# A gated mix of two attentions: the output and late-query products as 64-row halves inside the score bursts

## The chip, the cores and the metric

One core of one Trainium2 chip runs the whole program. The metric is device microseconds of that core, the median over several executions. Engines are called TensorE (PE, its weight loads PEld), VectorE (DVE), ScalarE (ACT), GpSimd (POOL) and SyncE (SP, which issues most DMAs).

## The reference

The output is `g * a + (1 - g) * b` for a sequence of 2048 tokens of 512 features, 32 heads of 16. All inputs and the output are float32.

```python
x = A_x                                                   # 1 x 2048 x 512
g = _sigmoid((x * gate_w).sum(-1, keepdims=True))
# a: full softmax attention
q, k, v = ((x @ wqkv) split into 3, by heads)
a = softmax(q k^T * 0.25) v, heads joined, @ A_wo
# b: four segments of 512 tokens, each attends causally to itself and reads a memory of the segments before it
for s in range(4):
    a_dot = softmax(qs ks^T * 0.25 + causal mask) vs
    a_mem = (phi(qs) M) / (phi(qs) z + 1e-6)              # phi(t) = t + 1 where t > 0, else exp(t)
    o_s   = sigmoid(beta) * a_mem + (1 - sigmoid(beta)) * a_dot
    M, z  = M + phi(ks)^T vs, z + sum(phi(ks))
b = (o_0 .. o_3 joined) @ B_wo
```

## The kernel before

A first phase (about 0 to 281 us) projects queries, keys and values, stores them to device memory, and builds the memory of side B. The attention follows, cut into units `(side, g, c)`: four heads `g`, one chunk `c` of 512 queries. Sides alternate, A then B, 32 of each. A unit of side A has 64 slots (`SLOTS`), one of side B has 10. A slot is one score tile: 128 keys by 512 queries of one head. Each slot does these things:

- `score_part(n)`: TensorE multiplies keys by queries into one of three rotating banks (`st`, line 1045), and ScalarE takes the exponential into a tile `p` (lines 1065 and 1068). On side B, GpSimd blanks what lies above the diagonal.
- `max_part(m)`, for the slot `LEAD` = 96 ahead: TensorE makes a tile with the operands exchanged (`sm`, line 242, four banks), and VectorE takes the row extremes (line 275, with a mask line 290). They are subtracted later inside the score product, through two additional rows of its operands.

Query and key tiles hold two heads in partitions 0 to 63 and two in 64 to 127. A product uses only 48 or 50 rows of one half. Score and maximum of one slot lie in opposite halves, so the two run side by side in TensorE.

Slots go in bursts of three (`BURST`). After each burst TensorE does something of another shape, which goes to the eighth bank, `ops`:

- `some_values(n, most(n))`: values times `p` (line 155, `ops<-p,vA` and `ops<-p,vB`, 128 rows by 17 columns, four heads side by side). `queue` holds slots whose exponentials are due; `most(n)` says how many are taken, three or four in most bursts. At a unit's end ScalarE copies `ops` to `oraw` (line 1106), and it is stored.
- Or, while the list `shared` holds anything, three items of it (line 155, 128 rows by 128 columns by 512). When side A's unit ends, `some_values` extends `shared` by twelve such products: either `output(...)`, half of one 128-token block of the final projection (operands `wA`, `wB` and `blk`; ended by `keep` or `leave`, which copy `ops` out on ScalarE, lines 1259 and 1263), or `later_tile(...)`, a query tile that the first phase left out (`ops<-wB,wA`, copy on line 962). Each logical product is three of high and low parts.

So twelve products take four bursts, during which no values are taken. The order is fixed in the program, each engine goes through its instructions in order, and waits follow from the tiles. `wait_early` ties the loads of the next burst to the last matmul of a burst; `run_late` transposes finished maxima. `wide`, the last 94 slots, is ordered otherwise, and the change does not touch it.

Of the kernel before, what the change touches and what calls it, by code (L numbers as in the profile page):

```python
# [10 lines left out]
F32 = mybir.dt.float32  # L11
F32R = mybir.dt.float32r
AF = mybir.ActivationFunctionType
ALU = mybir.AluOpType
# [8 lines left out]
CH = 512  # L23
# [11 lines left out]
LEAD = 96  # L35
BURST = 3
# [3 lines left out]
NP = 6  # L40
# [7 lines left out]
def gated_mix(ctx, tc, x, xT, wqkv, a_wo, b_wq, b_wk, b_wv, b_wo, beta, gate_w, out):  # L48
    nc = tc.nc
# [7 lines left out]
    for side in "AB":  # L57
        for o in range(NO):
            for c in range(NCH):
                rows_ = [32, 8, CH] if side == "A" else [2, 8, DH, CH]  # L60
# [22 lines left out]
                            compare_op=ALU.is_ge, fill=0.0)  # L83
    nc.gpsimd.affine_select(out=heads8, in_=heads8, pattern=[[DH, 8]], base=DH - 1, channel_multiplier=-1,
                            compare_op=ALU.is_ge, fill=0.0)
# [67 lines left out]
    def matmul(*args, **kw):  # L153

        behind[0] = nc.tensor.matmul(*args, **kw)  # L155
# [149 lines left out]
    def run_todo(m):  # L305

        for e in [e for e in todo if e[0] <= m]:
            todo.remove(e)
            e[1]()

    def run_late(pool, tag, m):
        while us := [e for e in late if e[0] < m][:2]:
            for e in us:
                late.remove(e)
            transpose_max(us, pool, tag)
# [639 lines left out]
    def x_later(c):  # L955
        return xT[:, c * CH:(c + 1) * CH]

    def later_tile(c, o):

        def done():  # L960
            full = fr.tile([128, CH], F32, tag="part", name="full")
            nc.scalar.copy(full, ops)
            t = fr.tile([128, 2, 2, 2, 128], F32R, tag="blk", name="qhalves", bufs=2)
            t = t.rearrange("p a o h t -> p a (o h t)")
            nc.gpsimd.tensor_copy(t[:, 0], full)
            nc.gpsimd.tensor_sub(t[:, 1], full, t[:, 0].bitcast(F32))
            for i in range(2):
                at(n + 12, lambda i=i: nc.sync.dma_start(
                    qd["A", o, c][16 * i:16 * i + 16].rearrange("d h t -> (d h) t"), raw(t[:, i])))


            if o == NO - 1 and c == LATER[0]:
                for i in range(2):
                    load_halves(("x", LATER[1]), "B", x_later(LATER[1]), (2 * i, 2 * i + 1), n + 2 + 18 * i,
                                [n + 24 + 29 * i, n + 28 + 29 * i])
            elif o == NO - 1:
                for i, (side, w) in enumerate((("A", a_wo), ("B", b_wo))):
                    load_halves(side, side, w, (0, 1), n + 2 + 18 * i, [n + 22 + 8 * i, n + 26 + 8 * i])
                    for k in range(2, 4):
                        load_halves(side, side, w, (k,), n + 50 + 22 * i + 3 * (k - 2), [n + 62 + 18 * i + 5 * (k - 2)])  # L980

        def f(i):
            k, (a, b) = i // 3, ((1, 0), (0, 1), (0, 0))[i % 3]
            assert {("q", k), (("x", c), k)} <= ready
            matmul(ops, halved["q"][:, k, a, o * 128:(o + 1) * 128], halved["x", c][:, k, b],
                             start=(i == 0), stop=(i == 11))
            if i == 11:
                done()
        for i in range(12):
            yield lambda i=i: f(i)  # L990

    vt = {}

# [33 lines left out]

    queue = []

    def score_part(n):  # L1030

        u, j = slots[n]
        side, g, c = u
        q = qt[u]

        if j % 4 == 0:
            pt_[u, j // 4] = pp.tile([128, 4, CH], F32, tag="p", name="p")
            order_p[u, j // 4] = len(order_p)
            assert not queue or order_p[queue[0][1], queue[0][2] // 4] > len(order_p) - 1 - NP
        p = pt_[u, j // 4]  # L1040
        h = (0, 2, 1, 3)[j % 4]

        def score(ps, h, b, k, n0, q0):

            nc.tensor.matmul(ps[:, n0:n0 + CH - q0], rows(k[:, :, b * 128:(b + 1) * 128], h, 50),  # L1045
                             rows(q[:, :, q0:], h, 50), start=True, stop=True)

        def diagonal(x):
            nc.gpsimd.affine_select(out=x, in_=x, pattern=[[0, 4], [1, 128]], base=0, channel_multiplier=-1,  # L1049
                                    compare_op=ALU.is_ge, fill=0.0)  # L1050

        ps = banks[1 + n % BURST] if n in wide and n // BURST % 2 else st_ps.tile([128, CH], F32, tag="st", name="st")
        if side == "A":
            score(ps, h, j // 4 % 4, kt_[u, j // 16], 0, 0)
        else:
            k = kt_[u, c]
            if j < 8:
                score(ps, h, j // 4, k, 0, 128 * (j // 4))
                if j >= 4:
                    score(ps, h, 3, k, 384, 384)  # L1060
            else:
                for f in range(2):
                    score(ps, 2 * (j - 8) + f, 2, k, 256 * f, 256)
        if side == "B" and j >= 8:
            nc.scalar.activation(p[:, 2 * (j - 8):2 * (j - 8) + 2, 0:256], ps.rearrange("p (h t) -> p h t", h=2), AF.Exp,
                                 scale=SCALE)
        else:
            nc.scalar.activation(p[:, h], ps, AF.Exp, scale=SCALE)  # L1068
        if j % 4 == 3 or j == SLOTS[side] - 1:
            if side == "B":  # L1070
                diagonal(p[:, :, 0:128])
                if j == 7:
                    diagonal(p[:, :, 384:])
            queue.extend((n + (2 * BURST * (1 + (side == "B")) if n in wide else GAP[side]), u, i) for i in range(j // 4 * 4, j + 1))


    PIECES = ([(0, 128 * i, 128 * i) for i in range(4)] + [(1, 128 * i, 128 + 128 * i) for i in range(3)] + [(3, 384, 384)]
# [137 lines left out]
    def products(ps, t, b, side, o, start, stop):  # L1215

        assert (side, o) in ready
        for i, (x, w) in enumerate(((1, 0), (0, 1), (0, 0))):
            yield lambda i=i, x=x, w=w: matmul(ps, t[:, b, x], halved[side][:, o, w], start=start and i == 0,
                                                         stop=stop and i == 2)  # L1220

    def out_rows(c, b):
        return out[c * CH + b * 128:c * CH + (b + 1) * 128, :]
# [17 lines left out]
    def output(c, b, pairs, then, ps=ops):  # L1241

        ks = [(os, o, i) for os in pairs for o in os for i in range(2)]
        for k in ks:
            def f(n, k=k):
                os, o, i = k
                assert loaded_blocks[c, b, os] > len(blocks) - 2
                t = blocks[loaded_blocks[c, b, os] - 1][:, i, o % 2].unsqueeze(1)
                list(products(ps, t, 0, "AB"[i], o, k == ks[0], k == ks[-1]))[n]()
                if k == ks[-1] and n == 2:  # L1250
                    then(ps, c, b)
            for n in range(3):
                yield lambda n=n, f=f: f(n)

    part = {}

# [57 lines left out]
    def most(n):  # L1314

        if not queue:
            return 0
        _, u, done = queue[0]
        side, left = u[0], SLOTS[u[0]] - done
        runs = (first[u] + SLOTS[side] + GAP[side] + 1 - n) // BURST  # L1320
        if side == "B" or runs < 1:
            return ends[side].get(left, MOST + (len(queue) > LOW))
        due = min(SLOTS[side], (n + BURST - GAP[side] - first[u] + 1) // 4 * 4) - done
        return MOST + (left - 4 >= (MOST + 0.5) * runs and (due > 2 * MOST or runs == 1))

    filled = [0]
    n = 0
    while n < nS or queue or beside or filled[0] < len(fill):
        for f in beside.pop(n, []):
            f()  # L1330
        if n < nS:
            score_part(n)
        m = n + LEAD
        if m < nS:
            loads(m + PRE)

            b = oldest()
            max_part(m, lambda: banks[b], b)
        run_todo(m)
        if n >= nS or n % (2 * BURST if n in wide else BURST) == (2 * BURST if n in wide else BURST) - 1:  # L1340
            taken = 0
            if shared:
                for _ in range(3):
                    shared.pop(0)()
            else:
                taken = some_values(n, 8 if n >= nS or n in wide else most(n))
            if n < 5:


                for i in range(4):  # L1350
                    nc.tensor.matmul(ops[:, 128 * i:128 * i + 128], identf, identf, start=True, stop=True)
            if any(e[0] < m + 1 for e in late):
                run_late(st_ps, "st", m + 1)
            else:

                for _ in range(0 if n >= nS and queue else 4 if n not in wide else 11 - taken if taken < 8 else 0):
                    if filled[0] == len(fill) or fill[filled[0]][0] > n:
                        break
                    fill[filled[0]][1]()
                    filled[0] += 1  # L1360
            if 5 < n < nS:
                wait_early(n)
        n += 1
# [45 lines left out]
```

## Time and profile before

| what | value |
|---|---|
| executions | 1745.94, 1745.3, 1744.92 us; median 1745.3 |
| profiled execution: span, first to last instruction | 1744.5 us |
| around the span, by the median | 0.8 us |
| busy: PE / DVE / ACT / POOL | 1738.4 / 1597.1 / 1436.5 / 736.5 us |
| matmuls and weight loads | 15205 each |
| output and late-query products in `ops` | 360 (132 + 132 + 96) |

No time of the profiled execution is listed apart from its span. In rows of the trace, `out<-in` names the tiles, then come partitions x elements and the count; times are in microseconds from the start of the span. Rows that merge several instructions show the time from the first one's start to the last one's end. Starts of TensorE's products are recorded, their ends are modelled.

### The profile page before, as it was taken

How to read it: one execution, taken by the hardware profiler on the slowest of the kernel's cores; microseconds unless marked ns; L12 is line 12 of the kernel's file. 1: busy time of each engine (PE TensorE's matmuls, PEld its weight loads, DVE VectorE, ACT ScalarE, POOL GpSimd, SP SyncE). 2: the span in 40 equal slices, each digit the busy share in tenths (PEclk: the TensorE clock that was granted, in tenths of full speed). 3: DMA queues.
4: the chain of work that ended last, by engine and by line, in shares of the span. 5: the costliest groups of instructions: out<-in, count | busy, mean ns of one | idle time of the engine just before them, and what ended most of it. 6: DMA issues, size and time to landing. Idle time of an engine off the chain costs nothing.

```text
span 1744.5 us, 41555 instructions
## 1 busy us (share of the span) xinstructions
PE 1738.4 (100%) x15205; PEld 885.8 (51%) x15205; DVE 1597.1 (92%) x3327; ACT 1436.5 (82%) x2763; POOL 736.5 (42%) x992
## 2 busy tenths in 40 slices
PE   9999999999999999999999999999999999999999
PEld 7887775444444444444444444444444444444445
DVE  7757788999999999999999999999999999999931
ACT  6545557888888898888888888888888888888884
POOL 3543233234352427352534353535344353535443
PEclk9999999999999999999999999999999999999999
DMA  6787567335453446454545454444445444545542
GB/s 209 251 291 227 194 226 215 110 102 145 127 153 105 138 119 183 131 137 136 143 122 157 122 143 130 134 145 122 149 130 148 130 127 124 148 115 147 149 154 63
DMA packets 149387, 261.62 MB, mean 150 GB/s; under 512 B 39064, under 2 KB 61624, under 8 KB 148672
## 3 DMA queue, kind: packets, MB, share of 16 engines
q1 hardware_dynamic: 146640, 254.42, 49.2%
q0 software_dynamic: 2400, 4.29, 0.9%
q8 instruction: 121, 1.98, 0.5%
q14 instruction: 82, 0.67, 0.1%
q10 hardware_dynamic: 144, 0.26, 0.1%
HBM read 174.39 MB, written 83.25 MB: 148 GB/s over the span
## 4 chain that ended last, share of the span: by engine, by line
PE 99%; ACT 0%; DMA 0%; DVE 0%; issue 0%; SPq 0%; ACTq 0%; DVEq 0%
PE ops L155 40%; PE st L1045 28%; PE sm L242 14%; PE pr L366 9%; PE pair L366 4%; PE sm L155 2%; PE mt_ps L232 0%; PE tps L831 0%; PE sm L1045 0%; DMA vs<-wqkv 0%; PE mps L845 0%; PE num L804 0%; PE den L808 0%; ACT p L1068 0%; DVE pm L275 0%
## 5 line engine op out<-in xcount | busy, mean ns | idle before, releaser
L1068 ACT ACTIVATE p<-st 128x512 f32<-128x512 f32 x2261 | 1190.7, 600 | 147.6 <-PE sm L242 98.6
L275 DVE TENSOR_REDUCE pm<-sm 128x1 f32<-128x512 f32 x2048 | 1276.5, 683 | 9.7 <-PE sm L242 8.7
L242 PE MATMUL sm<-kA,qA 48*128 48x512 f32 x2048 | 662.5, 424 | 0.1
L1045 PE MATMUL st<-qA,kA 50*128 50x512 f32 x2014 | 656.2, 432 | 0.0
L155 PE MATMUL ops<-p,vA 128*17 128x256 f32 (+3 forms) x6360 | 553.0, 445 | 0.0
L1045 PEld LDWEIGHTS st<-qA,kA 50*128 50x128 f32 x2014 | 326.8, 185 | 423.4 <-ACT p L1068 378.9
L242 PEld LDWEIGHTS sm<-kA,qA 48*128 48x128 f32 x2048 | 337.8, 185 | 11.3 <-DVE ph L449 3.9
L1169 POOL TENSOR_TENSOR rcp<-rec,minus 128x32 f32<-128x32 f32 x43 | 234.8, 5461 | 78.3 <-DMA rec<-dend 73.5
L290 DVE CUSTOM_DVE_ANT_0 rest<-sm,mask 128x128 f32<-128x128 f32 (+3 forms) x512 | 246.8, 482 | 0.8 <-PE sm L242 0.7
L155 PEld LDWEIGHTS ops<-p,vA 128*17 128x17 f32 x6360 | 129.2, 96 | 216.1 <-issue 185.0
L1049 POOL TENSOR_SCALAR_AFFINE_SELECT p<-p 128x512 f32<-128x512 f32 x128 | 79.4, 637 | 270.4 <-ACT p L1068 265.7
L242 PE MATMUL sm<-kB,qB 48*128 48x128 f32 (+3 forms) x512 | 166.1, 384 | 0.0
L1045 PE MATMUL st<-qB,kB 50*128 50x512 f32 (+1 forms) x495 | 105.4, 330 | 0.3 <-ACT mt L235 0.3
L1045 PEld LDWEIGHTS st<-qB,kB 50*128 50x128 f32 x495 | 68.6, 186 | 62.2 <-ACT p L1068 50.5
L155 PE MATMUL ops<-p,vB 128*17 128x128 f32 (+3 forms) x1504 | 88.3, 350 | 0.0
L242 PEld LDWEIGHTS sm<-kB,qB 48*128 48x128 f32 x512 | 79.9, 184 | 0.0
L214 POOL TENSOR_TENSOR dm<-pm 128x32 f32<-128x32 f32 x32 | 7.9, 247 | 169.9 <-DVE pm L275 169.9
L437 POOL TENSOR_SCALAR mn<-full 128x512 f32<-128x512 f32 x24 | 36.7, 1527 | 75.6 <-ACT full L432 75.6
L223 POOL CAST ms<-pm 128x16 fp32r<-128x16 f32 x32 | 6.3, 196 | 127.5 <-DVE pm L290 127.5
L1185 POOL TENSOR_TENSOR v<-v,inv 128x512 f32<-128x512 f32 x31 | 39.8, 1283 | 28.1 <-DMA inv<-rdA 21.9
L155 PEld LDWEIGHTS ops<-p,vB 128*17 128x17 f32 x1504 | 33.8, 96 | 30.1 <-issue 26.1
L440 DVE TENSOR_TENSOR q<-full,q 128x512 fp32r<-128x512 f32 x40 | 29.2, 731 | 18.6 <-ACT q L433 15.8
(319 smaller groups left out, 1690.9 us busy)
## 6 DMA issues: line engine op xcount, KB each, us to landing
kA<-kdA SPq DMA_DIRECT2D x256, 128.0 KB
vA<-vdA SPq DMA_DIRECT2D x31, 544.0 KB
kA<-kdA SPq DMA_DIRECT2D x256, 64.0 KB
qB<-qdB SPq DMA_DIRECT2D x192, 64.0 KB
kB<-kdB SPq DMA_DIRECT2D x192, 64.0 KB
kdA<-q SPq DMA_DIRECT2D x32, 256.0 KB
qdB<-q SPq DMA_DIRECT2D x32, 256.0 KB
qA<-qdA SPq DMA_DIRECT2D x64, 128.0 KB
```

What stands on the lines that cost most here:

```text
L155: behind[0] = nc.tensor.matmul(*args, **kw)
L242: nc.tensor.matmul(ps[:, n0:n0 + n], rows(qt[u][:, :, s * 128:(s + 1) * 128], h, 48), rows(k[:, :, k0:k0 + n], h, 48), start=True, stop=True)
L275: nc.vector.tensor_reduce(pm[:, h, s, kc:kc + 1], ps, axis=AX.X, op=ALU.max, negate=True)
L290: nc.vector.tensor_tensor_reduce(out=tri["rest"][:, 0:w], in0=ps[:, n0:n0 + w], in1=tri["mask"][:, CH - w:], scale=-1.0, scalar=3.0e38, op ...
L366: nc.tensor.matmul(ps, l, r, start=start, stop=stop)
L437: nc.gpsimd.tensor_scalar_min(ph["mn"], full, 0.0)
L440: nc.vector.tensor_sub(q2, full, q1.bitcast(F32))
L1045: nc.tensor.matmul(ps[:, n0:n0 + CH - q0], rows(k[:, :, b * 128:(b + 1) * 128], h, 50), rows(q[:, :, q0:], h, 50), start=True, stop=True)
L1049: nc.gpsimd.affine_select(out=x, in_=x, pattern=[[0, 4], [1, 128]], base=0, channel_multiplier=-1, compare_op=ALU.is_ge, fill=0.0)
L1068: nc.scalar.activation(p[:, h], ps, AF.Exp, scale=SCALE)
L1169: eng.tensor_tensor(r, rec, minus, op=ALU.pow)
L1185: eng.tensor_mul(k["v"], k["v"], k["inv"])
```

## The change

`shared` now holds functions of a row tile. `row_halves` cuts a product's contraction of 128 rows into two halves of 64 (`rs`), each a matmul of its own in row tile 0 or 1. All 24 halves of a set of twelve products accumulate in `ops`: the first has `start`, the last `stop`. When the row tile changes within a set, a `nc.tensor.drain()` stands ahead of the half, so that the two row tiles do not write one bank at the same time.

`output_burst(n)` takes a whole burst of three slots, and up to four products (`BURST + 1`) from `shared`. It sorts the three scores and three maxima by the row tile they use, and works in two phases: halves in row tile `one`, alternating with the scores and maxima of the other row tile; then the same exchanged. `turns` exchanges the first phase from burst to burst, so the next burst goes on in the row tile where the last one stopped. A set of twelve thus takes three bursts with one drain each. `score_part` is split into `score_tile` (allocation), `score_product` (product and exponential) and `score_values` (diagonal and `queue`). The main loop runs `output_burst` when `shared` is not empty at the start of a burst, and after every other burst takes values.

```diff
+    def row_halves(l, r, first_, last_, then=None):
+
+        def half(i):
+            rs = slice(64 * i, 64 * i + 64)
+            halves_done[0] += 1
+            if halves_done[0] > 1 and i != tile_of[0]:
+                nc.tensor.drain()
+            matmul(ops, l[rs], r[rs], start=halves_done[0] == 1, stop=halves_done[0] == 24)
+            tile_of[0] = i
+            if halves_done[0] == 24:
+                halves_done[0] = 0
+                if then:
+                    then()
+        return half
...
-            matmul(ops, halved["q"][:, k, a, o * 128:(o + 1) * 128], halved["x", c][:, k, b],
-                             start=(i == 0), stop=(i == 11))
-            if i == 11:
-                done()
+            return row_halves(halved["q"][:, k, a, o * 128:(o + 1) * 128], halved["x", c][:, k, b], i == 0, i == 11, done)
         for i in range(12):
-            yield lambda i=i: f(i)
+            yield lambda half, i=i: f(i)(half)
...
+    def score_half(n):
+
+        u, j = slots[n]
+        return (j - 8) if u[0] == "B" and j >= 8 else j % 2
...
+            if ps is ops:
+                yield row_halves(l, r, first_, last_)
+            else:
+                yield lambda l=l, r=r, first_=first_, last_=last_: matmul(ps, l, r, start=first_, stop=last_)
...
+            def half(i, n, f=f):
+                f(n)(i)
+                if not halves_done[0]:
+                    then(ps, c, b)
...
+    def maximum(n):
+
+        m = n + LEAD
+        if m < nS:
+            loads(m + PRE)
+
+            b = oldest()
+            max_part(m, lambda: banks[b], b)
+
+    def output_burst(n):
+
+        rows_ = [[], []]
+        for x in range(n, n + BURST):
+            score_tile(x)
+            r = score_half(x)
+            rows_[r].append(lambda x=x: score_product(x))
+            if x + LEAD < nS:
+                rows_[maxs[x + LEAD][1][0]].append(lambda x=x: maximum(x))
+        fs = [shared.pop(0) for _ in range(min(BURST + 1, len(shared)))]
+        one = turns[0] % 2
+        turns[0] += 1
+        for i, part in ((one, rows_[1 - one]), (1 - one, rows_[one])):
+            for k in range(max(len(fs), len(part))):
+                if k < len(fs):
+                    fs[k](i)
+                if k < len(part):
+                    part[k]()
+        for x in range(n, n + BURST):
+            score_values(x)
+
     n = 0
     while n < nS or queue or beside or filled[0] < len(fill):
         for f in beside.pop(n, []):
             f()
+        if shared and n % BURST == 0 and n < nS and n not in wide:
+            for _ in range(1, BURST):
+                n += 1
+                for f in beside.pop(n, []):
+                    f()
+            output_burst(n - BURST + 1)
+            run_todo(n + LEAD)
+            m = n + LEAD
+            if any(e[0] < m + 1 for e in late):
+                run_late(st_ps, "st", m + 1)
+            wait_early(n)
+            n += 1
+            continue
         if n < nS:
-            score_part(n)
+            score_tile(n)
+            score_product(n)
+            score_values(n)
...
-            taken = 0
-            if shared:
-                for _ in range(3):
-                    shared.pop(0)()
-            else:
-                taken = some_values(n, 8 if n >= nS or n in wide else most(n))
+            taken = some_values(n, 8 if n >= nS or n in wide else most(n))
```

More of the change, by code (lines that the diff above doesn't have):

```diff
@@ L956, in x_later @@
         return xT[:, c * CH:(c + 1) * CH]
+    halves_done = [0]
+    tile_of = [0]
+    def row_halves(l, r, first_, last_, then=None):
[11 more added lines that the diff above has]
+        return half
     def later_tile(c, o):
@@ L1028, in gated_mix, with score_tile @@
     queue = []
-    def score_part(n):
+    def score_tile(n):
         u, j = slots[n]
-        side, g, c = u
-        q = qt[u]
         if j % 4 == 0:
@@ L1039, in score_part, with score_product @@
             assert not queue or order_p[queue[0][1], queue[0][2] // 4] > len(order_p) - 1 - NP
+    def score_product(n):
+        u, j = slots[n]
+        side, g, c = u
+        q = qt[u]
         p = pt_[u, j // 4]
@@ L1046, in score @@
                              rows(q[:, :, q0:], h, 50), start=True, stop=True)
-        def diagonal(x):
-            nc.gpsimd.affine_select(out=x, in_=x, pattern=[[0, 4], [1, 128]], base=0, channel_multiplier=-1,
-                                    compare_op=ALU.is_ge, fill=0.0)
         ps = banks[1 + n % BURST] if n in wide and n // BURST % 2 else st_ps.tile([128, CH], F32, tag="st", name="st")
@@ L1068, in score_part, with score_values, diagonal @@
             nc.scalar.activation(p[:, h], ps, AF.Exp, scale=SCALE)
+    def score_values(n):
+        u, j = slots[n]
+        side = u[0]
+        p = pt_[u, j // 4]
+        def diagonal(x):
+            nc.gpsimd.affine_select(out=x, in_=x, pattern=[[0, 4], [1, 128]], base=0, channel_multiplier=-1,
+                                    compare_op=ALU.is_ge, fill=0.0)
         if j % 4 == 3 or j == SLOTS[side] - 1:
@@ L1074, in score_part @@
             queue.extend((n + (2 * BURST * (1 + (side == "B")) if n in wide else GAP[side]), u, i) for i in range(j // 4 * 4, j + 1))
+    def score_half(n):
+        u, j = slots[n]
+        return (j - 8) if u[0] == "B" and j >= 8 else j % 2
     PIECES = ([(0, 128 * i, 128 * i) for i in range(4)] + [(1, 128 * i, 128 + 128 * i) for i in range(3)] + [(3, 384, 384)]
@@ L1218, in products @@
         for i, (x, w) in enumerate(((1, 0), (0, 1), (0, 0))):
-            yield lambda i=i, x=x, w=w: matmul(ps, t[:, b, x], halved[side][:, o, w], start=start and i == 0,
-                                                         stop=stop and i == 2)
+            l, r, first_, last_ = t[:, b, x], halved[side][:, o, w], start and i == 0, stop and i == 2
+            if ps is ops:
+                yield row_halves(l, r, first_, last_)
+            else:
+                yield lambda l=l, r=r, first_=first_, last_=last_: matmul(ps, l, r, start=first_, stop=last_)
     def out_rows(c, b):
@@ L1248, in f, with both @@
                 t = blocks[loaded_blocks[c, b, os] - 1][:, i, o % 2].unsqueeze(1)
-                list(products(ps, t, 0, "AB"[i], o, k == ks[0], k == ks[-1]))[n]()
+                return list(products(ps, t, 0, "AB"[i], o, k == ks[0], k == ks[-1]))[n]
+            def both(n, f=f, k=k):
+                f(n)()
                 if k == ks[-1] and n == 2:
                     then(ps, c, b)
+            def half(i, n, f=f):
+                f(n)(i)
+                if not halves_done[0]:
+                    then(ps, c, b)
             for n in range(3):
-                yield lambda n=n, f=f: f(n)
+                yield (lambda i, n=n, half=half: half(i, n)) if ps is ops else lambda n=n, both=both: both(n)
     part = {}
@@ L1326, in gated_mix @@
     filled = [0]
[L1327 to L1331, printed above, removed]
-            score_part(n)
+    turns = [0]
+    def maximum(n):
         m = n + LEAD
@@ L1338, in gated_mix @@
             max_part(m, lambda: banks[b], b)
+    def output_burst(n):
[17 more added lines that the diff above has]
+            score_values(x)
+    n = 0
+    while n < nS or queue or beside or filled[0] < len(fill):
+        for f in beside.pop(n, []):
[3 more added lines that the diff above has]
+                n += 1
+                for f in beside.pop(n, []):
+                    f()
+            output_burst(n - BURST + 1)
[6 more added lines that the diff above has]
+            continue
+        if n < nS:
+            score_tile(n)
+            score_product(n)
+            score_values(n)
+        m = n + LEAD
+        maximum(n)
         run_todo(m)
         if n >= nS or n % (2 * BURST if n in wide else BURST) == (2 * BURST if n in wide else BURST) - 1:
-            taken = 0
-            if shared:
-                for _ in range(3):
-                    shared.pop(0)()
-            else:
-                taken = some_values(n, 8 if n >= nS or n in wide else most(n))
+            taken = some_values(n, 8 if n >= nS or n in wide else most(n))
             if n < 5:
```

## The prediction

> **What bounds the kernel now.** I began with the page: the span, the busy shares and the chain that ended last.
>
> ```profile
> span 1744.5 us, 41555 instructions
> PE 1738.4 (100%) x15205; PEld 885.8 (51%) x15205; DVE 1597.1 (92%) x3327; ACT 1436.5 (82%) x2763; POOL 736.5 (42%) x992
> PE 99%; ACT 0%; DMA 0%; DVE 0%; issue 0%; SPq 0%; ACTq 0%; DVEq 0%
> ```
>
> TensorE carries 99% of the chain, but a busy TensorE is no proof, since the ends of its products are modelled. So next come a window of the steady part and, from the groups by line, VectorE's share of it.
>
> ```profile
> 400.00:1600.00 1200.00, 1199.95 (x11256) 547.00 (x11252) 1198.65 (x2556) 1070.21 (x2073) 526.02 (x715) 1.00 0.48 136
> L275 DVE TENSOR_REDUCE pm<-sm 128x1 f32<-128x512 f32 x1698 | 1057.4, 683 | 0.6
> ```
>
> The columns are window, length, then the busy time of TensorE, weight loads, VectorE, ScalarE and GpSimd, the clock (1.00, so no throttle enters), DMA share and GB/s. VectorE is busy for 1198.65 of 1200 us as well: two engines are close to full. A faster TensorE would soon meet VectorE, while a slower one has no cover. Which of the two sets the pace is read from TensorE's own timeline around one unit's output products:
>
> ```profile
> 818.92 1.05 PE L155 MATMUL ops<-p,vA 128*17 128x512 f32 x8
> 819.91 0.50 PE L242 MATMUL sm<-kA,qA 48*128 48x512 f32 x1
> 820.25 0.45 PE L242 MATMUL sm<-kA,qA 48*128 48x512 f32 x1
> 820.87 0.96 PE L155 MATMUL ops<-wA,blk 128*128 128x512 f32 x3
> 821.75 0.44 PE L1045 MATMUL st<-qB,kB 50*128 50x384 f32 x1
> 822.71 0.96 PE L155 MATMUL ops<-wB,blk 128*128 128x512 f32 x3
> 824.55 0.97 PE L155 MATMUL ops<-wA,blk 128*128 128x512 f32 x3
> 826.39 0.96 PE L155 MATMUL ops<-wB,blk 128*128 128x512 f32 x3
> 827.28 0.50 PE L1045 MATMUL st<-qA,kA 50*128 50x512 f32 x1
> 827.28 0.50 PE L242 MATMUL sm<-kA,qA 48*128 48x512 f32 x1
> 827.62 0.40 PE L1045 MATMUL st<-qA,kA 50*128 50x512 f32 x1
> 827.62 0.40 PE L242 MATMUL sm<-kA,qA 48*128 48x512 f32 x1
> 827.86 0.40 PE L1045 MATMUL st<-qA,kA 50*128 50x512 f32 x1
> 827.86 0.40 PE L242 MATMUL sm<-kA,qA 48*128 48x512 f32 x1
> 828.18 0.84 PE L155 MATMUL ops<-p,vB 128*17 128x384 f32 x8
> 828.95 0.50 PE L1045 MATMUL st<-qA,kA 50*128 50x512 f32 x1
> 835.44 1.05 PE L155 MATMUL ops<-p,vA 128*17 128x512 f32 x8
> 836.43 0.50 PE L1045 MATMUL st<-qA,kA 50*128 50x512 f32 x1
> 837.33 1.05 PE L155 MATMUL ops<-p,vA 128*17 128x512 f32 x8
> ```
>
> A score product (st) and a maximum product (sm) start in the same instant, one in rows 0 to 63 and one in rows 64 to 127, so three slots are three pairs. Their starts are 0.34, then 0.24, then 0.32 us apart (827.28, 827.62, 827.86, 828.18): a product costs 0.24, and going into and out of another shape costs 0.10 and 0.08, together 0.18 a switch. One row stretch of pairs takes 0.90 (827.28 to 828.18, 836.43 to 837.33), three full-row output products 0.89 (826.39 to 827.28), three slots' values 0.77 (828.18 to 828.95), four 0.99 (835.44 to 836.43). These intervals fit 0.24 a product with nothing over: TensorE issues without waiting, and is the bound here. I call a stretch of pairs T, values V and output products O.
>
> **The change part by part.** How often it happens follows from the groups by shape:
>
> ```profile
> L155 PE MATMUL ops<-wB,blk 128*128 128x512 f32 x132 | 42.4, 429 | 0.0
> L155 PE MATMUL ops<-wA,blk 128*128 128x512 f32 x132 | 42.3, 428 | 0.0
> L155 PE MATMUL ops<-wB,wA 128*128 128x512 f32 x96 | 30.8, 429 | 0.0
> ```
>
> That listing gives 132 + 132 + 96 = 360 products in sets of 12: 30 units. Now a unit spends T O T O T O T O T between two values, 819.91 to 828.18 = 8.27 us. Afterwards it spends three mixed bursts and one T; one T and one V burst more follow elsewhere, because the set takes three bursts of slots and not four.
>
> *Removed: switches; added: halves.* A mixed burst has eight half products beside six pair products; each row tile sees 4 + 3 in each of two phases, so the longer side is 8 x 0.24. Three bursts are 24 products: 0.34 + 23 x 0.24 = 5.86 us. The T behind them needs no switch in: 0.24 + 0.24 + 0.32 = 0.80.
>
> *The extra burst.* The number of values is unchanged. Four cost 0.99 and three 0.77, 0.22 each, so a V burst costs 0.77 - 3 x 0.22 = 0.11 by itself; with its T of 0.90 that is +1.01.
>
> *The drain, three a unit, 90 in all.* No row shows one under load. The nearest rows:
>
> ```profile
> L1383 PEldq DRAIN  x2: 13/2145/4277, 1736.3 to 1744.0; - x2
> 827.42 0.60 ACT L1263 COPY res<-ops 128x512 f32<-128x512 f32 x1
> PEld ops L155 <- issue: 231.1, 753, 0.7
> ```
>
> On an empty array a drain took 13 ns: the lower end (it can bring no gain, since it only orders). Under load it must wait for the last half product, 0.40 long of which 0.24 is the usual pitch: 0.16. The end must be noticed: the last output product's record ends at 826.39 + 0.96 = 827.35, and ScalarE reads at 827.42, 0.07 later. Then weights that could not be loaded ahead: 0.10, as after a switch. Together 0.33; I take 0.34. For the upper end I add the idle time in which weight loads wait on issue alone, 231.1 / 753 = 0.31: 0.64. It also holds back scores and maxima of the second phase.
>
> The Trainium skill, TensorE: Matmul & The Clock Gate (Single matmul latency), gives a lone warm product (398 + N) / 2.4 ns, for 512 columns an estimated 379 ns; the trace has 0.40 us, so they agree within 6%. By the page alone, a drain would cost its 0.38 less the 0.24 pitch, 0.14, and the 90 drains 13 us where I take 31.
>
> *A wait that is new, at the first half.* All these products share the bank ops with the values. When a unit's values are done, ScalarE copies ops out, and only then may the first output product overwrite it:
>
> ```profile
> 820.04 0.59 ACT L1106 COPY oraw<-ops 128x512 f32<-128x512 f32 x1
> ```
>
> The copy ends at 820.63. Today T covers it: the output products start at 820.87. In the new order the first half product is the very next matmul after the values, at 819.91. It must wait until 820.63 plus the 0.07 of notice, 820.70: 0.79 us. TensorE takes its instructions in order, so all scores and maxima of that burst queue behind it, ScalarE's exponentials and VectorE's reductions behind those. Bounds: 0.72 (no notice) to 0.96 (the present 820.87).
>
> *The copy out at the end.* Today it starts at 827.42, when ScalarE has no exponentials left, and ends at 828.02 before V at 828.18. In the mixed burst one or two exponentials of the last phase stand before it. I take 0.15 us of delay to the next V; bounds 0 to 0.40, two thirds of a 0.60 us operation.
>
> *Recovered.* VectorE loses nothing that TensorE does not lose first, but banks now come free earlier than needed, so small waits of T (0.96 at 819.91 against 0.90) may shrink. I credit 0.2 us a unit, between 0 and 0.4. DMAs, GpSimd's splits and stores are the same ones, one burst earlier; SP's and GpSimd's queues are not passed. I cost them at nothing: the output block is asked for 20 slots ahead of the unit's end, about 12 us at 1.84 us for three slots (822.71 to 824.55).
>
> *Sum.* After: 0.79 + 5.86 + 3 x 0.34 + 0.80 + 0.15 = 8.62. Against 8.27 that is +0.35; with the extra burst +1.36, less 0.20 = +1.16 a unit. Times 30: +35 us. The runs' median, 1745.3, stands 0.8 above the span that I sum against, so I forecast 1780 us.
>
> **The rivals.** Without the drains, the first wait and the late copy, a unit would be 0.60 faster, 0.80 with the recovery: this is what the removed switches are worth, and everything turns on what replaces them.
>
> *Cheap drain.* If it costs 0.013 to 0.20, the sum falls by 0.42 to 0.98 a unit: +0.18 to +0.74, so 1751 to 1767. For: the 13 ns row. Against: that array was empty. The Trainium skill, VectorE: DVE Perf Modes (The DRAIN you can't avoid), calls drains of about 12 ns, constant, boilerplate on all engines; the trace's 13 ns agrees, but no row here shows such a drain behind a running product.
>
> *No first wait; the other side.* If the wait holds only the one half product, or the copy comes earlier, 0.79 goes: +0.37, 1756 us. It turns to faster when in addition the drain is below (0.80 - 0.15) / 3 = 0.22; at 0.18, the switch's price, it is -0.11 a unit, 1742. For: nothing but the short drain. Against: copy and first product are adjacent in TensorE's order, and the copy runs 0.72 us past 819.91.
>
> *VectorE is the true bound.* Then TensorE's additions vanish into its slack and nothing moves, 1745. For: 1198.65 of 1200 us. Against: T, O and V keep their lengths with no stretching.
>
> *The halves don't run beside the pairs.* Then each phase costs seven products and not four: 6 x 3 x 0.24 = 4.3 us more a unit, 130 us in all, 1910. Against: the pairs at 827.28, 827.62 and 827.86, which use the same two row tiles.
>
> **How the numbers follow.** Forecast (1767 to 1808) 0.66; cheap drain 0.13; no first wait 0.13, of it 0.08 faster; VectorE's bound 0.04, of it 0.01 faster; no pairing 0.04. Slower by over 0.2% is 0.66 + 0.13 + 0.05 + 0.04 = 0.88, faster 0.09, within it 0.03; 0.2%, 3.5 us, is about what a measurement of this kernel can tell from no change. The upper end sets all drains at 0.64 (27 us more, 1807); the lower, 1752, takes in the cheap drain and the missing wait. Left out are about 0.16.
>
> **What would show it.** After the last values of a unit, TensorE's first half product should start about 0.8 us late, released by ScalarE's copy L1106, with weight loads put down to it in the list of waits. Between the two phases of each mixed burst the starts should stand about 0.6 us apart (0.24 + 0.34). Mixed bursts should last 8 x 0.24 + 0.34 = 2.26 us, the first 0.9 more; VectorE's busy time in the steady window should fall to about 97%. I am wrong if the phases join at 0.3 us, or if the first half starts on time.

## The result and the profile after

The changed kernel takes 1809.98 us (1809.06 to 1810.49) against 1745.11 for the one before: ratio 1.037, 95% interval 1.0355 to 1.0385. It is slower by 65 us; the forecast was 35 us slower, and 1810 lies 2 us above the range.

The page's span, busy shares and chain of the changed kernel:

```profile
span 1808.1 us, 43943 instructions
PE 1771.2 (98%) x16365; PEld 952.0 (53%) x16365; DVE 1608.6 (89%) x3327; ACT 1453.3 (80%) x2763; POOL 737.4 (41%) x992
PE 95%; ACT 3%; issue 1%; DMA 1%; SPq 0%; DVE 0%; ACTq 0%; DVEq 0%
```

The same window as before, columns as there:

```profile
400.00:1600.00 1200.00, 1173.03 (x11722) 574.58 (x11722) 1154.47 (x2439) 1035.63 (x1979) 498.74 (x685) 1.00 0.46 130
```

VectorE's total work is nearly unchanged (1597.1 and 1608.6 us busy on the two pages), but in the window it falls from 1198.65 to 1154.47 us: it now idles. ScalarE appears in the chain with 3%. TensorE's timeline around the unit that the prediction showed:

```profile
844.19 1.05 PE L155 MATMUL ops<-p,vA 128*17 128x512 f32 x8
845.95 0.49 PE L155 MATMUL ops<-wA,blk 64*128 64x512 f32 x1 [0.71 <-ACT oraw L1136]
...
846.74 0.39 PE L155 MATMUL ops<-wB,blk 64*128 64x512 f32 x1
847.22 0.49 PE L155 MATMUL ops<-wA,blk 64*128 64x512 f32 x1
847.22 0.50 PE L242 MATMUL sm<-kA,qA 48*128 48x512 f32 x1
847.55 0.39 PE L155 MATMUL ops<-wA,blk 64*128 64x512 f32 x1
...
848.95 0.39 PE L155 MATMUL ops<-wA,blk 64*128 64x512 f32 x1
849.42 0.50 PE L155 MATMUL ops<-wB,blk 64*128 64x512 f32 x1
...
852.42 0.39 PE L155 MATMUL ops<-wB,blk 64*128 64x512 f32 x1
...
853.43 0.49 PE L242 MATMUL sm<-kA,qA 48*128 48x512 f32 x1
853.85 0.86 PE L155 MATMUL ops<-p,vB 128*17 128x384 f32 x8
```

The halves do run beside the pairs: a half and a maximum both start at 847.22. The first half product waits for ScalarE's copy of ops (the bracket is TensorE's idle time and what ended it). Between phases stand 0.48 (846.74 to 847.22) and 0.47 us (848.95 to 849.42), with one drain in each; over all 90 drains the mean is 0.47.

To see where the time went I cut each unit at TensorE's starts: the *region* runs from the start of the last values product of a unit of side A to the start of the next values, the *rest* from there to the next region. T, as in the prediction, is one stretch of three pairs. All means are over 29 units.

| per unit, us | before | after | difference |
|---|---|---|---|
| region | 8.79 | 9.20 | +0.40 |
| rest | 36.41 | 38.14 | +1.73 |
| of it, stretches of pairs T: number x mean length | 19.7 x 0.918 | 20.7 x 0.942 | +1.42: one more T, 0.92, and longer ones, 0.50 |
| three-value and four-value bursts | 8.8 and 10.9 | 12.8 and 7.9 | +0.17 without the single stop below |

Thirty times 0.40 + 0.92 + 0.17 + 0.50 is 60 us. One unit alone (its rest begins at 660 us) is about 4 us longer than its like, 3.5 more than the same unit before. The remaining 1 to 2 us are not assigned.

### The profile page after: what moved, and what is told of

Read it like the earlier page. It is cut to its first block, busy times and chain, and to the rows that moved or that the text cites. A ratio compares the mean times of both kernels' runs of the same rounds, so it can differ in the third digit from the quotient of the medians.

```text
span 1808.1 us, 43943 instructions
## 1 busy us (share of the span) xinstructions
PE 1771.2 (98%) x16365; PEld 952.0 (53%) x16365; DVE 1608.6 (89%) x3327; ACT 1453.3 (80%) x2763; POOL 737.4 (41%) x992
## 4 chain that ended last, share of the span: by engine, by line
PE 95%; ACT 3%; issue 1%; DMA 1%; SPq 0%; DVE 0%; ACTq 0%; DVEq 0%
PE ops L155 40%; PE st L1063 24%; PE sm L242 14%; PE pr L366 9%; PE pair L366 4%; ACT p L1082 2%; PE sm L155 2%; ACT oraw L1136 1%; PE mt_ps L232 0%; PE tps L831 0%; PE sm L1063 0%; SPq L174 0%; DMA vs<-wqkv 0%; PE mps L845 0%; DMA rdA<-rec 0%
## 5 line engine op out<-in xcount | busy, mean ns | idle before, releaser
L242 PE MATMUL sm<-kA,qA 48*128 48x512 f32 x2048 | 706.9, 432 | 0.1
L1063 PE MATMUL st<-qA,kA 50*128 50x512 f32 x2014 | 667.2, 433 | 0.0
L155 PE MATMUL ops<-p,vA 128*17 128x256 f32 (+3 forms) x7160 | 560.0, 414 | 2.0 <-DMA rec<-odB 2.0
L155 PEld LDWEIGHTS ops<-p,vA 128*17 128x17 f32 x7160 | 149.6, 96 | 224.5 <-issue 185.5
L290 DVE CUSTOM_DVE_ANT_0 rest<-sm,mask 128x128 f32<-128x128 f32 (+3 forms) x512 | 246.4, 481 | 10.9 <-PE sm L242 8.6
L1063 PE MATMUL st<-qB,kB 50*128 50x512 f32 (+1 forms) x495 | 121.1, 324 | 0.3 <-ACT mt L235 0.3
L155 PE MATMUL ops<-wA,blk 64*128 64x512 f32 x264 | 85.5, 416 | 18.9 <-ACT oraw L1136 15.3
L1063 PEld LDWEIGHTS st<-qB,kB 50*128 50x128 f32 x495 | 86.6, 186 | 17.2 <-ACT p L1082 15.2
L155 PE MATMUL ops<-wB,blk 64*128 64x512 f32 x264 | 81.0, 399 | 1.8
L155 PEld LDWEIGHTS ops<-wA,blk 64*128 64x128 f32 x264 | 45.4, 184 | 60.0 <-ACT oraw L1136 35.6
```

The lines of the kernel that those rows point to most:

```text
L242: nc.tensor.matmul(ps[:, n0:n0 + n], rows(qt[u][:, :, s * 128:(s + 1) * 128], h, 48), rows(k[:, :, k0:k0 + n], h, 48), start=True, stop=True)
L290: nc.vector.tensor_tensor_reduce(out=tri["rest"][:, 0:w], in0=ps[:, n0:n0 + w], in1=tri["mask"][:, CH - w:], scale=-1.0, scalar=3.0e38, op ...
```

## The experiments

Two theories for what the prediction had missed, the longer T in the rest. Theory A: VectorE is starved in the mixed bursts, and since it was nearly full before, it becomes the bound afterwards. Theory B: the stretching belongs to TensorE's own order.

**E1, only the regrouping: four full-row products a burst, no halves.** In the kernel before:

```diff
             if shared:
-                for _ in range(3):
+                for _ in range(4):
                     shared.pop(0)()
```

> The kernel before with one number changed: four full-row products a burst instead of three, so a set of twelve takes three bursts and no product is halved. TensorE alone: a unit's region loses one T (0.92) and one switch (0.18) and a little more, the rest gains one T and one values burst (1.01): about -0.2 a unit, 1739 us. Theory A (VectorE is the second bound and cannot catch up after a stretch of starvation): a T with four products lasts 2.04 us against VectorE's need of 1.80, the 0.7 us of starvation a unit is mostly within its backlog, so 1741 to 1749. If either holds, regrouping four by three is not what costs 65 us, and the halving is. If regrouping itself is the cause (one more values burst a unit), 1790 or more.

Measured: 1759.85 us, ratio 1.0081 (1.0067 to 1.0095). None of the estimates held: 14 us slower. The region gained 1.09 a unit (7.70 for 8.79), as counted, but the rest grew by 1.52 (37.94): the extra T and values burst, T 0.932 long on average, and one stop of 3.4 us in a single unit. So of the 65 us, 14 come with the regrouping and 50 with the halving, its wait and its drains.

**E2, a burst of plain pairs ahead of each set**, so that the copy of ops has cover, and the set again takes four bursts' slots:

```diff
     def output_burst(n):
 
+        if not begun[0]:
+            begun[0] = True
+            for x in range(n, n + BURST):
+                score_tile(x)
+                score_product(x)
+                score_values(x)
+                maximum(x)
+            return
...
         fs = [shared.pop(0) for _ in range(min(BURST + 1, len(shared)))]
+        begun[0] = bool(shared)
```

> The changed kernel with one burst of plain pairs, without values, ahead of each set, so that ScalarE's copy of ops runs behind these pairs. The wait of 0.77 at the first half goes, a T of 0.82 takes its place, and the extra T and values burst (1.09) goes back. Theory A (the stretching of T in the rest of the unit, 0.50, comes from VectorE that was starved in the mixed bursts): this goes too, -1.54 a unit, 1764 us. Theory B (the stretching belongs to TensorE's own order and stays): -1.04 a unit, 1779 us. If the first wait was no loss: 1800 or more.

Measured: 1764.99 us, ratio 1.011 (1.0096 to 1.0124): theory A's 1764, 14 us from B's. The rest is back at 36.39 (36.41 before) and VectorE is nearly full again. Since the set takes four bursts' slots again, the rest also has its former mix of values bursts, so E2 alone doesn't tell whether VectorE or the mix made T longer. Its row of the same window:

```profile
400.00:1600.00 1200.00, 1191.92 (x11430) 567.04 (x11426) 1190.06 (x2517) 1062.78 (x2044) 520.49 (x712) 1.00 0.46 134
```

What remains is in the region, 9.44 for 8.79. This is what halving costs with the wait covered. I put it down to three drains and a late copy, less the switches saved; the parts were not measured one by one.

**E3, three products a mixed burst, four bursts a set:**

```diff
-        fs = [shared.pop(0) for _ in range(min(BURST + 1, len(shared)))]
+        fs = [shared.pop(0) for _ in range(min(BURST, len(shared)))]
```

> The changed kernel with three products a mixed burst instead of four: four mixed bursts a set, each phase three halves beside three pair products. The 24 halves keep their pitch, there is one drain more (+0.24 a unit), the first wait stays, and the extra T and values burst goes (-1.09). Theory A: the stretching goes as well, since VectorE gets twelve slots' maxima in the mixed bursts and not nine: -1.35 a unit, 1770 us. Theory B: -0.85 a unit, 1784 us.

Measured: 1794.52 us, ratio 1.0279 (1.0265 to 1.0293). A miss for both. The rest did return to 36.30 a unit, so the longer T was gone, but the region took 10.51. One term is the drain: there are four a set, not three, and each is dearer. With four halves against three pair products, the last half of a phase runs alone; with three against three, a pair product starts just behind it, and the drain waits for that too. TensorE's timeline of E3:

```profile
838.29 0.38 PE L155 MATMUL ops<-wA,blk 64*128 64x512 f32 x1
838.52 0.39 PE L155 MATMUL ops<-wA,blk 64*128 64x512 f32 x1
838.54 0.44 PE L242 MATMUL sm<-kA,qA 48*128 48x512 f32 x1
839.09 0.50 PE L155 MATMUL ops<-wA,blk 64*128 64x512 f32 x1
```

The phases stand 0.57 apart here (838.52 to 839.09) and 0.59 on average over 120 drains, not 0.47. From the first half to the last a set takes 7.28 us for 6.46. The other term lies at the end of the set, where the time from the last half to the next values went from 1.45 to 1.94 us: scores there wait for banks that ScalarE still holds, behind the copy out.

```profile
845.75 0.58 ACT L1304 COPY res<-ops 128x512 f32<-128x512 f32 x1
846.89 0.50 PE L1063 MATMUL st<-qA,kA 50*128 50x512 f32 x1 [0.47 <-ACT p L1082]
```

**E4, one drain more in each mixed burst, amid the first phase:**

```diff
-            if halves_done[0] > 1 and i != tile_of[0]:
+            if halves_done[0] > 1 and (i != tile_of[0] or halves_done[0] % 8 == 3):
                 nc.tensor.drain()
```

> The changed kernel with one drain more in each mixed burst, between the second and third half of its first phase, 90 in all; nothing else differs. By the starts in the changed kernel's trace a drain costs 0.24: +21 us, 1831. By the prediction's 0.34: +31, 1841. By a drain that costs next to nothing: 1811. If VectorE's later limit hid it: less than 1820.

Measured: 1846.73 us, ratio 1.0579 (1.0564 to 1.0593), 36.8 more than the changed kernel, 0.41 for each of 90. The region grew by 1.18 a unit, 0.39 a drain. That is above my 0.24, which had counted only the gap and not the 0.10 that the next pair loses (0.33 for 0.23, at 847.22 to 847.55), and near the prediction's 0.34. The starts around an added drain stand 0.53 apart on average, between the 0.47 of a drain behind a lone half and the 0.59 of E3: an amid-phase drain has a pair product to wait for, as in E3. The cheap drain is excluded.

**E5, E6, E7: VectorE relieved.** In the kernel before, the changed one and E1, the maximum reads 384 of 512 columns, so side A's maxima leave out a quarter of the keys:

```diff
-            nc.vector.tensor_reduce(pm[:, h, s, kc:kc + 1], ps, axis=AX.X, op=ALU.max, negate=True)
+            nc.vector.tensor_reduce(pm[:, h, s, kc:kc + 1], ps[:, 0:384], axis=AX.X, op=ALU.max, negate=True)
```

> The kernel before, with VectorE's maximum over 384 of the 512 columns (side A's maxima thus leave out a quarter of the keys); TensorE's work is the same. It takes VectorE's limit away, by an estimated 0.13 us a slot from the 512 columns in 0.60. Theory A: only the small stretching of T goes (0.918 to 0.905 on average, 0.3 a unit), 1736 us. Theory B: 1745.

> The same shortening in the changed kernel. Theory A (the rest of a unit is held up by VectorE, which was starved in the mixed bursts): the stretching of T goes, 0.5 to 0.6 a unit, 1793 us, and the distance to the shortened kernel before falls from 65 to about 57. Theory B (TensorE's own order): 1807 to 1810, distance 65 or more. The first wait and the drains, on TensorE, stay by both.

> The same shortening in the kernel before with four full-row products a burst. Theory A: the stretching of T in the rest goes, about 0.35 a unit, 1749 us, which is what TensorE alone should make of the regrouping less what a values burst costs. Theory B: 1759.

Measured, with the ratio to the kernel before: E5 1741.69 us, 0.9976 (0.9966 to 0.9985); E6 1793.73, 1.0275 (1.0259 to 1.029); E7 1747.36, 1.0009 (0.9999 to 1.0018). E6 and E7 came out near theory A, 1793 and 1749, and far from theory B; E5 gained 4 us, between the two. The same window for E6:

```profile
400.00:1600.00 1200.00, 1172.03 (x11822) 565.35 (x11820) 996.94 (x2459) 1043.22 (x1994) 503.80 (x683) 1.00 0.44 130
```

VectorE has about 200 us to spare there, and T in the rest falls from 0.942 to 0.921, as before the change. E7 does the same to E1's T: 0.932 falls to 0.919. So it is VectorE that lengthens T.

That it does so because it was starved in the mixed bursts is not shown. From the gaps between its starts, VectorE idles 0.6 us a unit in the region of E1, 2.0 in the changed kernel and 3.3 in E4, while T in the rest is 0.932, 0.942 and 0.943; in E3 it idles 1.2 us and T is 0.915. T is longer in the kernels that regroup twelve products into three bursts, and so have about four three-value bursts more a unit, and not in E2 and E3, which have as many as before. More than half of the longer T (0.932 of 0.942, from 0.918) comes with the regrouping alone.

The split by engine follows from the same runs. The distance from before to after falls from 65 to 52 us: 52 us that TensorE would lose with VectorE out of the way (6 for the regrouping, E7 less E5, and 46 for the halving, E6 less E7), and 13 us go through VectorE. The single stop stands in E6 and E7 (4 to 5 us) but not in E5, so most of the 6 is that stop, and little is left for the regrouping itself. The window of E5 tells why the kernel before is no better off: TensorE stays full while VectorE falls to 1030 us, and the time hardly moves.

```profile
400.00:1600.00 1200.00, 1200.00 (x11241) 545.65 (x11239) 1030.49 (x2556) 1071.04 (x2075) 523.32 (x715) 1.00 0.46 136
```

No version tried is faster than the kernel before, apart from E5, which computes less.

## Why the prediction was wrong

The direction and the likeliest case were right, the size was not. Point by point:

- *First wait, 0.79 us:* 0.77 measured on average, released by ScalarE's copy as said. In the list of waits of the window, the line of weight loads that wait for that copy grows; before and after:

```profile
PEld ops L155 <- ACT oraw L1106: 11.3, 35, 0.4
PEld ops L155 <- ACT oraw L1136: 51.0, 51, 1.6
```

- *Drain, 0.34 us:* the gap 0.48 less the pitch 0.23, and 0.10 at the next pair: 0.34 to 0.35. The Trainium skill's latency of a lone product (TensorE: Matmul & The Clock Gate, Single matmul latency), an estimated 379 ns by its formula, agrees again with the 0.39 of these halves, though their ends are modelled and so no independent measure. The tail alone, 0.14, is less than half of what a drain costs here. The drains of about 12 ns that the Trainium skill, VectorE: DVE Perf Modes (The DRAIN you can't avoid), describes as boilerplate are no guide for one behind running products. The prediction said that no row of the trace before shows such a drain, but its own row lists two: the other, of 4277 ns from 1736.3 on, stood behind products and ended with the last of them.
- *Twenty-four halves:* 6.46 us from the first to the last, plus 0.23, is 6.69, against 5.86 + 1.02 with the drains. The pitch was 0.23, not 0.24.
- *Late copy, 0.15 us:* too small. From the last half to the values 1.45 us passed, where 0.24 + 0.80 + 0.15 = 1.19 were allowed. The copy began 0.62 after the last half (0.48 before), behind exponentials of the last phase.
- *Region together:* +0.35 forecast, +0.40 measured. That it is so close is partly luck: the last two terms, -0.19 and +0.26, nearly cancel.
- *Extra burst, +1.01:* 0.92 + 0.17 = 1.09.
- *Recovered, -0.20:* this step failed. It was +0.50. I had written that VectorE loses nothing that TensorE does not lose first, and that banks would come free early. In fact, VectorE idles 2.0 us a unit in the region (0.1 before), from the gaps between its starts, and with only four banks between the engines it can't run far behind or ahead. And about four more bursts a unit now hold three values rather than four, faster than VectorE's three maxima. There TensorE waits for VectorE. From the trace of the changed kernel, just after a set:

```profile
854.64 0.50 PE L1063 MATMUL st<-qA,kA 50*128 50x512 f32 x1
855.42 0.18 PEld L242 LDWEIGHTS sm<-kA,qA 48*128 48x128 f32 x1 [0.18 <-DVE pm L290]
855.85 0.84 PE L155 MATMUL ops<-p,vB 128*17 128x128 f32 x16
856.63 0.50 PE L1063 MATMUL st<-qA,kA 50*128 50x512 f32 x1
857.65 1.06 PE L155 MATMUL ops<-p,vB 128*17 128x128 f32 x24
855.29 4.27 DVE L275 TENSOR_REDUCE pm<-sm 128x1 f32<-128x512 f32 x7
```

The weight load for a maximum product sits until VectorE has read the bank. The first T here lasts from 854.64 to 855.85, 1.21 us, but the T at the same place took 1.05 before (828.95 to 830.00). The clearer one is the next, from 856.63 to 857.65: 1.02, where the kernel before has 0.90:

```profile
830.77 0.50 PE L1045 MATMUL st<-qA,kA 50*128 50x512 f32 x1
831.67 1.06 PE L155 MATMUL ops<-p,vB 128*17 128x128 f32 x24
```

VectorE goes through its seven maxima without a gap, (4.27 - 0.68) / 6 = 0.60 from start to start, so three take 1.80 us; and that is what TensorE's three values and T take together, 855.85 to 857.65. E6 and E7 show that VectorE is the cause; the larger share comes with the regrouping, as E1 shows. The step is worth (0.50 + 0.20) x 30 = 21 us of the 30 that were missed.

- *The single stop:* 3.5 to 4 us. The prediction cost DMAs and the queues of SyncE and GpSimd at nothing, as the same ones, one burst earlier; that failed too. The timeline shows TensorE stopping in the middle of a group of sixteen values products:

```profile
687.01 1.05 PE L155 MATMUL ops<-p,vA 128*17 128x128 f32 x14
690.06 0.81 PE L155 MATMUL ops<-p,vA 128*17 128x384 f32 x2 [1.99 <-DMA rec<-odB]
```

Fourteen had gone, and two came 2.5 us after them. The release named is a load that these products do not read; but they are the last of a burst, to which `wait_early` ties the loads of the next burst. Those loads, `qB` and `kB`, were issued only from 682.16 on, after SyncE had stood 6.4 us, until 673.43, for GpSimd's split of `wA`:

```profile
SPq L944 <- POOL wA L949: 6.4, 1, 6.4
673.43 0.38 SPq L944 DMA_DIRECT2D wraws<-b_wo  x1
682.16 2.92 SPq L174 DMA_DIRECT2D qB<-qdB  x6
685.12 2.96 SPq L174 DMA_DIRECT2D kB<-kdB  x6
```

E1, E4, E6 and E7 stop near the same unit and have the same wait of SyncE (5.8 to 6.4 us); the kernel before, E2 and E5 have neither, and E3 has 1.3 us of it and no stop. No run took that wait away, so the chain is read from the traces and not tested.

Of the rivals, the missing wait, the cheap drain and the missing pairing are refuted. The rival that VectorE is the true bound was half right: not for the kernel before (E5 moved it by 4 us), but as a ceiling in the rest of each unit after the change.

## What to carry to other kernels

When two engines are both near 100%, ask of each burst which of them it favours: an order that is cheaper for the first, here three values for four, may ask more of the second than it can do. Ask also how much backlog lies between them, here four banks, before crediting the first with catching up. Before putting products at the front of a burst, look at what reads their bank last: the stretch that a change removes may have been the cover of a copy. And cost a regrouping by what the other bursts become: three bursts for four meant more bursts of three values, and 14 us by itself, 3 of them the stop. Last, cost the queues too: one burst earlier was enough to make a load wait.

## What the runs showed of the hardware

A drain on TensorE costs by what runs when it comes: 0.24 us of gap when the last product is alone (0.47 less 0.23), 0.34 (0.57 less 0.23) when a product in the other row tile started 0.02 later, and in both cases 0.10 more at the next pair. Against this stand the 0.18 us that a switch of shape takes in these traces, without a drain in the program. A set trades its switches, about 0.6 us by the prediction's sum, for three drains of 0.34, 1.02 together, which is a loss before the first wait and the late copy are added.
